# A two-branch linear-attention block: x's first 256 rows by transposing transfers, the first weights on one queue

## The chip, the cores and the metric

The kernel runs on one core of a Trainium2 chip. The metric is the device time of one execution in microseconds (us), lower is better. A profiled execution gives, beside its time, a span: from the first instruction that the profiler sees to the last.

## What is computed

The input x has 2048 rows of 640 numbers in bf16. Two linear-attention blocks A and B, each with its own weights, are applied to the same x, and a gate mixes their outputs row by row.

```python
def block(x, wqkv, wo):                       # 32 heads of 20
    q, k, v = split(x @ wqkv)                 # x: 2048x640, wqkv: 640x1920
    phi = lambda t: where(t > 0, t + 1, exp(t)) + 1e-6
    pq, pk = phi(q), phi(k)
    kv = einsum("bhsd,bhse->bhde", pk, v)     # per head 20x20
    z = einsum("bhsd->bhd", pk)
    o = einsum("bhqd,bhde->bhqe", pq, kv) / (einsum("bhqd,bhd->bhq", pq, z)[..., None] + 1e-6)
    return merge_heads(o) @ wo
g = sigmoid((x * gate_w).sum(-1, keepdims=True))
out = g * block(x, A_wqkv, A_wo) + (1 - g) * block(x, B_wqkv, B_wo)
```

## The kernel before

TensorE multiplies with the contracted dimension on the 128 partitions, so nearly everything needs x transposed: the tile `xT` holds it as 5 column groups (`c`) of 128 features by 2048 rows. The tile `xn` holds x as it is, 16 chunks of 128 rows, for later products with `pk`. Key weights of block A are in `wkA` (`wk[0]`, 5 groups by 640 columns, and two columns more, of which the first is filled with the gate weight), query weights in `wqA`, value weights in `wvA`.

The work starts with `k_first`: keys of block A for the first four row chunks. Each chunk takes 10 products on line 340 (5 groups `c` times two halves `hf` of the columns), added up in a bank pair `kA`. The second half is 321 columns wide: its last column is the gate. So the gate weights, loaded as 5 rows into the tile `g5` (`g` in the profile), are transposed by one small TensorE instruction (line 268, `gate_column`), and ScalarE copies them in three pieces into `wkA` (line 270) before any product with the second half can start.

Ahead of `k_first`, seven products of constants (`warm`, line 254) keep TensorE busy while the first transfers are on their way. Behind it come the first query products of block A (`qA`, lines 750 and 390) and from there an order written out by hand (the table `FIRST`), in which key chunks and query units follow each other to the end of the span's first third. Each engine works its list off in order.

How x's first rows come into `xT`: chunks 0 and 1 are loaded as they are into `xn` (line 200), one from SyncE's queue (SP) and one from ScalarE's (ACT); `x_transpose` lets TensorE transpose each by 5 products with the identity (line 295) into PSUM, and VectorE copies the result in two pieces to `xT` (line 298). Chunks 2 and 3 come by one transposing transfer of 256 whole rows (line 206, SP), rows 512 to 1023 by five transposing transfers of one column group each, the rest by two of 512 whole rows, all on SP. The key weights are loaded in pieces of 1, 1, 1 and 2 groups (line 203): the first, third and fourth from SP, the second from ACT. The gate weights come behind it on ACT. Chunks 2 and 3 are loaded into `xn` once more, untransposed, behind all of these (line 1313), then the other twelve (line 1315).

An instruction that starts a transfer occupies its queue for the time of the issue; the bytes land later. A queue's transfers wait in line for the 16 DMA engines, which both queues share.

Of the kernel before, what the change touches and what calls it, by code (L numbers as in the profile page):

```python
# [9 lines left out]
P = 128  # L10
# [5 lines left out]
S, D, H = 2048, 640, 32  # L16
Dh = D // H
DT = D // P
ST = S // P
NB = 4  # L20
CB = 4
HB = 512
# [56 lines left out]
def kernel(  # L79
# [11 lines left out]
    nc = tc.nc  # L91
    x2 = A_x.flatten_outer_dims()
# [28 lines left out]
    def ps_raw(name, slot=None):  # L121

        if slot is None:
            slot = turn[0]
            turn[0] = (slot + 1) % 4
        return pools.get(slot, pools["ps"]).tile([P, 4 * HB], BF16, tag=f"ps{slot}", name=name)

    def banks(raw):

        return raw.bitcast(FP32).rearrange("p (b n) -> p b n", b=2)  # L130

    def ps(name, slot=None):

        return banks(ps_raw(name, slot))

    xT = persist.tile([P, DT, S], BF16, name="xT")
    xn = persist.tile([P, ST, D], BF16, name="xn")
# [6 lines left out]
    ident = persist.tile([P, P], BF16, name="ident")  # L144
# [46 lines left out]
    nc.vector.memset(tiny[:], LOGS * EPS)  # L191
    nc.vector.memset(maskE[:], 1.0)
    nc.vector.memset(E4[0:2 * H, HF:D], 0.0)
    xb0 = x2[0:CB * P, :].rearrange("(q p) d -> p q d", p=P)
    wk = [None, None]
    wv = [None, None]
    wq = [None, None]
    wk[0] = wpool.tile([P, DT, D + 2], BF16, tag="wk", name="wkA")
    def load_x(eng, lo, hi):
        eng.dma_start(out=xn[:, lo:hi, :], in_=xb0[:, lo:hi, :])  # L200

    def load_wk(eng, lo, hi):
        eng.dma_start(out=wk[0][:, lo:hi, 0:D], in_=wq_dram[0][:, lo:hi, D:2 * D])

    def load_xT(lo, hi, c0=0, c1=DT):
        nc.sync.dma_start_transpose(out=xT[:, c0:c1, lo:hi], in_=x2[lo:hi, c0 * P:c1 * P])

    wq[0] = wpool.tile([P, DT, D], BF16, tag="wq", name="wqA")
    with tc.manual_schedule():
        load_x(nc.sync, 0, 1)  # L210
        load_x(nc.scalar, 1, 2)
        load_wk(nc.sync, 0, 1)
        load_wk(nc.scalar, 1, 2)
        nc.scalar.dma_start(out=g5[:], in_=gate_w.rearrange("(c p) -> c p", p=P))
        load_wk(nc.sync, 2, 3)
        load_wk(nc.sync, 3, DT)
        load_xT(HB // 2, HB)
        nc.scalar.preload_act_table_set("natural_log_exp_and_others")
        for lo, hi in ((0, 2), (2, 4), (4, DT)):
            nc.sync.dma_start(out=wq[0][:, lo:hi, :], in_=wq_dram[0][:, lo:hi, 0:D])  # L220
        for c in range(DT):
            load_xT(HB, 2 * HB, c, c + 1)
        for n in range(2, NB):
            load_xT(n * HB, (n + 1) * HB)
# [3 lines left out]
    for r in range(4):  # L228
# [3 lines left out]
        out=spread[:].rearrange("p (h t) -> p h t", t=TW), in_=I4[:, :, None].to_broadcast([P, H, TW])  # L232
    )
    for lo in range(0, HF, K6):
        part = maskE[:, lo:min(lo + K6, HF)]
        for sign, base in ((1, 0), (-1, Dh - 1)):
            nc.gpsimd.affine_select(
                out=part, in_=part, pattern=[[-sign * Dh, part.shape[1] // Dh], [0, Dh]],
# [3 lines left out]
    for rows, n in ((slice(0, 2 * H), H // 2), (slice(2 * H, P), H)):  # L242
        nc.gpsimd.tensor_copy(
            out=E4_rows[rows, 0:n], in_=I4[rows, 0:n, None].to_broadcast([rows.stop - rows.start, n, Dh])
# [20 lines left out]
    def gate_column(pt):  # L265

        at = slice(4 * HB - 2 * P, 4 * HB - 2 * P + DT)
        nc.tensor.transpose(out=pt[:, at], in_=g5[:], identity=ident[0:DT, 0:DT])
        for lo, hi in ((0, 1), (1, 2), (2, DT)):
            nc.scalar.copy(out=wk[0][:, lo:hi, D:D + 1], in_=pt[:, at, None][:, lo:hi])  # L270
# [18 lines left out]
                out=ge[32 * j:32 * j + 32], in_=by_rows[j][None].to_broadcast([H, 2, HB])  # L289
            )  # L290

    def x_transpose(i, slot):
        pt = ps_raw("xt", slot)
        for c in range(DT):
            nc.tensor.transpose(out=pt[:, c * P:(c + 1) * P], in_=xn[:, i, c * P:(c + 1) * P], identity=ident[:])
        src = pt[:, 0:D].rearrange("p (c n) -> p c n", c=DT)
        for lo, hi in ((0, 2), (2, DT)):
            nc.vector.tensor_copy(out=xT[:, lo:hi, i * P:(i + 1) * P], in_=src[:, lo:hi])

    class Phi:  # L300

        def __init__(self, dst, src, lifted=False):
# [35 lines left out]
    def k_mm(b, i, c, pt, hf):  # L338
        n = HF + (b == 0 and hf == 1)
        nc.tensor.matmul(  # L340
            pt[:, hf, 0:n], lhsT=xT[:, c, i * P:(i + 1) * P], rhs=wk[b][:, c, hf * HF:hf * HF + n],
            start=(c == 0), stop=(c == DT - 1),
        )
# [17 lines left out]
    def k_first():  # L361

        pts = []

        def part(i, cs, hfs=(0, 1)):
            for c in cs:
                for hf in hfs:
                    k_mm(0, i, c, pts[i], hf)

        x_transpose(0, 3)  # L370
        x_transpose(1, 2)
        gate_column(warm_raw)
        pts += [ps("kA", 1), ps("kA", 3)]
        for hf in range(2):
            for i in range(2):
                part(i, (0, 1), (hf,))
        for cs in ((2,), (3, 4)):
            for i in range(2):
                part(i, cs)
        pts += [ps("kA", 0), ps("kA", 2)]  # L380
        for i in range(2, CB):
            part(i, range(DT))
        return pts
# [148 lines left out]
    class PhiSteps:  # L532
# [9 lines left out]
        def part(self, t, k):  # L542
            return t if len(self.srcs) == 1 else t[:, k]
# [766 lines left out]

    with tc.manual_schedule():
        pts = k_first()
        nc.sync.dma_start(out=xn[:, 2:CB, :], in_=xb0[:, 2:CB, :])
        for n in range(1, NB):
            nc.sync.dma_start(
                out=xn[:, n * CB:(n + 1) * CB, :], in_=x2[n * HB:(n + 1) * HB, :].rearrange("(q p) d -> p q d", p=P)
            )
# [3 lines left out]
        lo, hi = GT  # L1321
# [197 lines left out]
        part = [slice(n * RB, (n + 1) * RB) for n in range(4)]  # L1519
# [70 lines left out]
        for i in range(1, half):  # L1590
            p, after = pairs[i], pairs[i + 1] if i + 1 < half else None
# [7 lines left out]
            q = after if i + 2 < half else p if after is None else None  # L1599
# [42 lines left out]
```

## Time and profile before

| | |
|---|---|
| time, median of 3 runs | 181.27 us (180.89, 181.27, 181.69) |
| profiled execution: its own time and its span | 180.88 us, 179.2 us |
| TensorE (PE) busy | 175.1 us, 98% of the span, 1266 products |
| VectorE (DVE) busy | 151.1 us, 84% |
| ScalarE (ACT) busy | 112.4 us, 63% |
| GpSimd (POOL) busy | 4.4 us, 2% |
| moved by DMA | 19.18 MB, mean 107 GB/s |

The profiled execution ran 0.39 us below the median, and 1.7 us of its time lie outside of its span. The busy time of TensorE counts overlapping products once; it says that TensorE is the engine that the others keep up with, not that it runs at its peak. PEld is the loading of the stationary operand, which runs beside the products.

### The profile page before, as it was taken

What the parts mean: (1) busy time and instruction counts of PE and PEld (TensorE: products, weight loads), DVE (VectorE), ACT (ScalarE), POOL (GpSimd) and SP (SyncE); (2) the same over time, 40 slices, a digit from 0 to 9 for tenths busy, and PEclk for the clock granted to TensorE, in tenths of its full rate; (3) what the DMA queues carried; (4) which work ended last, traced back from release to release, by engine and by line L of the source; (5) the groups of instructions that cost most, each with busy time, mean ns of one, the idle gap of its engine ahead of it and who ended that gap; (6) DMA issues with size and microseconds to landing.
All of it is one profiled execution on the core that took longest, in us unless ns stands there. A gap on an engine that the chain in (4) does not pass through costs nothing.

```text
span 179.2 us, 3362 instructions
## 1 busy us (share of the span) xinstructions
PE 175.1 (98%) x1266; PEld 116.2 (65%) x1266; DVE 151.1 (84%) x283; ACT 112.4 (63%) x235; POOL 4.4 (2%) x19
## 2 busy tenths in 40 slices
PE   7999999999999999999999999999999999999993
PEld 3666665665666577565656676766678777777772
DVE  2389999999999986898999997987988988686774
ACT  2388978999652453686869677674715756456410
POOL 7100000000000000000000000000000000000000
PEclk9999999999999999999999999999999999999999
DMA  5999999406045033000000033234802560233132
GB/s 174 293 188 178 214 366 316 108 4 183 3 125 180 0 116 121 0 0 0 2 4 2 0 72 114 57 103 157 233 3 70 145 154 0 74 113 113 73 134 90
DMA packets 22642, 19.18 MB, mean 107 GB/s; under 512 B 10338, under 2 KB 22114, under 8 KB 22626
## 3 DMA queue, kind: packets, MB, share of 16 engines
q1 hardware_dynamic: 22040, 18.47, 37.4%
q10 hardware_dynamic: 586, 0.49, 0.9%
q8 instruction: 10, 0.16, 0.4%
q14 instruction: 6, 0.05, 0.1%
HBM read 11.86 MB, written 4.80 MB: 93 GB/s over the span
## 4 chain that ended last, share of the span: by engine, by line
PE 95%; DMA 2%; DVE 1%; ACTq 0%; issue 0%
PE q L524 16%; PE kA L340 12%; PE kB L340 9%; PE gs L842 9%; PE gs L1331 9%; PE oy L1126 6%; PE oz L1126 5%; PE ox L1126 5%; PE ow L1126 4%; PE kB L524 3%; PE gB L812 2%; PE gA L812 2%; PE qA L390 2%; DMA g<-in_gate_w_dram 2%; PE q L390 1%; PE qA L750 1%
## 5 line engine op out<-in xcount | busy, mean ns | idle before, releaser
L340 PEld LDWEIGHTS <-xT 128*128 128x128 bf16 x280 | 27.1, 97 | 15.1 <-DMA xT<-in_A_x_dram 0.3
L340 PE MATMUL kA<-wkA,xT 128*128 128x320 bf16 (+1 forms) x160 | 24.0, 299 | 0.0
L554 DVE TENSOR_SCALAR e<-e 128x640 bf16<-128x640 bf16 (+2 forms) x59 | 19.2, 335 | 4.8 <-ACT e L548 4.5
L548 ACT ACTIVATE e<-q 128x512 bf16<-128x512 f32 x32 | 18.5, 599 | 5.7 <-PE q L524 5.2
L340 PE MATMUL kB<-wkB,xT 128*128 128x320 bf16 x120 | 19.2, 299 | 0.0
L548 ACT ACTIVATE e<-kB 128x640 bf16<-128x640 f32 (+1 forms) x18 | 11.4, 647 | 7.3 <-PE kB L524 3.2
L548 ACT ACTIVATE e<-kA 128x640 bf16<-128x640 f32 x16 | 11.3, 712 | 4.5 <-PE kA L340 3.8
L530 DVE TENSOR_TENSOR q<-q,p 128x512 f32<-128x512 f32 x16 | 11.1, 696 | 1.7 <-PE q L524 1.2
L561 DVE SCALAR_TENSOR_TENSOR pk<-kB,e 128x640 bf16<-128x640 f32 (+1 forms) x16 | 11.6, 736 | 0.5
L1126 PEld LDWEIGHTS <-xT 128*128 128x128 bf16 x85 | 8.1, 98 | 2.9
L1126 PEld LDWEIGHTS <-pqTA 128*128 128x128 bf16 x85 | 8.0, 98 | 2.8
L1126 PEld LDWEIGHTS <-pqTB 128*128 128x128 bf16 x80 | 7.8, 98 | 3.0
L524 PE MATMUL q<-xT,wqB 128*128 128x512 bf16 x32 | 9.7, 379 | 0.0
L1189 ACT COPY u<-ox 128x320 f32<-128x320 f32 x8 | 3.4, 425 | 9.7 <-PE ox L1126 9.7
L1131 DVE TENSOR_TENSOR osb<-oz,u 128x320 bf16<-128x320 f32 (+2 forms) x18 | 7.9, 451 | 1.9 <-PE oz L1126 1.6
L524 PE MATMUL q<-SQ,TM 128*128 128x512 bf16 x32 | 8.5, 379 | 0.0
L1331 PEld LDWEIGHTS <-xn 128*128 128x128 bf16 x64 | 6.1, 98 | 3.1 <-issue 0.7
L812 PEld LDWEIGHTS <-xn 128*128 128x128 bf16 x64 | 6.2, 98 | 2.8
L842 PEld LDWEIGHTS <-xn 128*128 128x128 bf16 x64 | 6.1, 98 | 2.9 <-issue 0.7
L561 DVE SCALAR_TENSOR_TENSOR pk<-kA,e 128x640 bf16<-128x640 f32 x8 | 6.6, 822 | 0.4
L561 DVE SCALAR_TENSOR_TENSOR pqTB<-q,e 128x512 bf16<-128x512 f32 x10 | 6.7, 683 | 0.0
L1126 PE MATMUL oz<-MB,xT 128*128 128x320 bf16 (+2 forms) x45 | 6.8, 284 | 0.0
(205 smaller groups left out, 372.6 us busy)
## 6 DMA issues: line engine op xcount, KB each, us to landing
out_dram<-osb SPq DMA_DIRECT2D x14, 160.0 KB, 1.8
xn<-in_A_x_dram SPq DMA_DIRECT2D x3, 640.0 KB, 7.8
wvA<-in_A_wqkv_dram SPq DMA_DIRECT2D x1, 800.0 KB, 10.4
wkB<-in_B_wqkv_dram SPq DMA_DIRECT2D x1, 800.0 KB, 4.6
wqB<-in_B_wqkv_dram SPq DMA_DIRECT2D x1, 800.0 KB, 5.8
wvB<-in_B_wqkv_dram SPq DMA_DIRECT2D x1, 800.0 KB
MA<-m_rows SPq DMA_DIRECT2D x1, 800.0 KB, 4.7
MB<-m_rows SPq DMA_DIRECT2D x2, 400.0 KB, 4.8
```

Of the source, the lines that this page charges most:

```text
L340: nc.tensor.matmul(pt[:, hf, 0:n], lhsT=xT[:, c, i * P:(i + 1) * P], rhs=wk[b][:, c, hf * HF:hf * HF + n], start=(c == 0), stop=(c == DT - 1),
L390: nc.tensor.matmul(dst, lhsT=mixed(wq[b][:, c, :], m), rhs=xT[:, c, n * HB:(n + 1) * HB], start=first, stop=last,)
L524: nc.tensor.matmul(dst, lhsT=left(c), rhs=right(c), start=first and k == 0, stop=last and k == len(cs) - 1, skip_group_check=not first,)
L530: nc.vector.tensor_tensor(out=dst, in0=acc, in1=sb, op=ALU.add)
L548: nc.scalar.activation(out=self.part(self.e, k), in_=self.srcs[k](), func=ACT.Exp)
L554: nc.vector.tensor_scalar(self.e, self.e, 1.0, EPS, op0=ALU.min, op1=ALU.add)
L561: nc.vector.scalar_tensor_tensor(out=self.part(self.dst, k), in0=src(), scalar=1.0 + EPS, in1=self.part(self.e, k), op0=ALU.add, op1=ALU.max,)
L812: nc.tensor.matmul(pt[:, hf, 0:HF], lhsT=xn[:, i, c * P:(c + 1) * P], rhs=pk[:, i, hf * HF:(hf + 1) * HF], start=(i == 0), stop=(i == ST - 1),
L842: nc.tensor.matmul(pt[:, n, 0:HF], lhsT=left[:, i, n * P:(n + 1) * P], rhs=right[:, i, :], start=(first and i == 0), stop=(i == hc - 1), s ...
L1126: nc.tensor.matmul(dst, lhsT=left[:, c, r0:r0 + P], rhs=right[:, c, :], start=(first and c == 0), stop=(c == DT - 1), skip_group_check=not ...
L1131: nc.vector.tensor_tensor(out=dst, in0=acc, in1=sb, op=ALU.add)
L1331: nc.tensor.matmul(dst[n], lhsT=left[:, i, n * P:(n + 1) * P], rhs=right[:, i, :], start=(first and i == 0), stop=(i == hc - 1), skip_grou ...
```

## The change

Three things are changed, all at the start of the program. The first 256 rows of x come into `xT` by two transposing transfers of 128 whole rows, at the head of SP's queue; `x_transpose`, its ten TensorE products and four VectorE copies are gone. All four pieces of the key weights and the gate weights are issued by ACT, in the order first and second piece, gate, third and fourth piece. And `k_first` has another order: two products of chunk 0's first half stand ahead of the gate's transposition, its second half and all of chunk 1 behind. The untransposed copy of chunks 0 and 1 in `xn` is loaded later, with chunks 2 and 3 in one transfer of 640 KB.

```diff
-    xb0 = x2[0:CB * P, :].rearrange("(q p) d -> p q d", p=P)
-    def load_x(eng, lo, hi):
-        eng.dma_start(out=xn[:, lo:hi, :], in_=xb0[:, lo:hi, :])
...
-        load_x(nc.sync, 0, 1)
-        load_x(nc.scalar, 1, 2)
-        load_wk(nc.sync, 0, 1)
+        load_xT(0, P)
+        load_wk(nc.scalar, 0, 1)
         load_wk(nc.scalar, 1, 2)
         nc.scalar.dma_start(out=g5[:], in_=gate_w.rearrange("(c p) -> c p", p=P))
-        load_wk(nc.sync, 2, 3)
-        load_wk(nc.sync, 3, DT)
-        load_xT(HB // 2, HB)
+        load_xT(P, 2 * P)
+        load_wk(nc.scalar, 2, 3)
+        load_wk(nc.scalar, 3, DT)
+        load_xT(2 * P, HB)
...
-    def x_transpose(i, slot):
-        pt = ps_raw("xt", slot)
-        for c in range(DT):
-            nc.tensor.transpose(out=pt[:, c * P:(c + 1) * P], in_=xn[:, i, c * P:(c + 1) * P], identity=ident[:])
-        src = pt[:, 0:D].rearrange("p (c n) -> p c n", c=DT)
-        for lo, hi in ((0, 2), (2, DT)):
-            nc.vector.tensor_copy(out=xT[:, lo:hi, i * P:(i + 1) * P], in_=src[:, lo:hi])
...
-        x_transpose(0, 3)
-        x_transpose(1, 2)
+        pts += [ps("kA", 1), ps("kA", 3)]
+        part(0, (0, 1), (0,))
         gate_column(warm_raw)
-        pts += [ps("kA", 1), ps("kA", 3)]
+        part(0, (0, 1), (1,))
         for hf in range(2):
-            for i in range(2):
-                part(i, (0, 1), (hf,))
+            part(1, (0, 1), (hf,))
...
-        nc.sync.dma_start(out=xn[:, 2:CB, :], in_=xb0[:, 2:CB, :])
-        for n in range(1, NB):
+        for n in range(NB):
```

On TensorE, right behind the `warm` products, this stood before (the end of the second chunk's transposition, the gate's transposition, the first key products; a DMAHW semaphore is the landing of one transfer, DVE, PE and Activation are work of these engines):

```order
L295 MATMUL xt<-ident,xn 128x128
L268 LDWEIGHTS g_89 [waits DMAHW4_49]
L268 MATMUL warm<-ident,g_89 128x5
L340 LDWEIGHTS xT [waits DVE_49]
L340 MATMUL kA<-wkA,xT 128x320 [waits DMAHW3_49]
L340 LDWEIGHTS xT
L340 MATMUL kA<-wkA,xT 128x320 [waits DMAHW2_49]
```

The gate's transposition came ahead of all key products, and four products of the first half stood between it and the first product that needs its column. At the same place, directly behind the last `warm` product, the changed program has (its line 328 is line 340 of before, 264 is 268):

```order
L328 LDWEIGHTS xT [waits DMAHW1_49]
L328 MATMUL kA<-wkA,xT 128x320 [waits DMAHW0_49]
L328 LDWEIGHTS xT
L328 MATMUL kA<-wkA,xT 128x320 [waits DMAHW2_49]
L264 LDWEIGHTS g_89 [waits DMAHW4_49]
L264 MATMUL warm<-ident,g_89 128x5 [waits Pool_49]
L328 LDWEIGHTS xT
L328 MATMUL kA<-wkA,xT 128x321 [waits Activation_49]
```

Two key products moved ahead of the gate, and the product right behind it now waits for ScalarE's copy.

SP's queue from its start, before:

```order
L200 DMA xn<-in_A_x_dram 128x640
L203 DMA wkA<-in_A_wqkv_dram 128x640 x2
L203 DMA wkA<-in_A_wqkv_dram 128x2x640
L206 DMA_TRANSPOSE xT<-in_A_x_dram 128x5x256
L220 DMA wqA<-in_A_wqkv_dram 128x2x640 [waits DMAHW0_49]
L220 DMA wqA<-in_A_wqkv_dram 128x2x640 [waits DMAHW1_49]
```

Four plain transfers stood ahead of the transposing one. The same queue in the changed program:

```order
L202 DMA_TRANSPOSE xT<-in_A_x_dram 128x5x128 x2
L202 DMA_TRANSPOSE xT<-in_A_x_dram 128x5x256
L216 DMA wqA<-in_A_wqkv_dram 128x2x640 [waits DMAHW0_49]
L216 DMA wqA<-in_A_wqkv_dram 128x2x640 [waits DMAHW1_49]
L216 DMA wqA<-in_A_wqkv_dram 128x640 [waits DMAHW2_49]
```

Only transposing transfers are left ahead of the query weights. ACT's queue in the changed program, from its start to the gate's copies:

```order
L199 DMA wkA<-in_A_wqkv_dram 128x640 x2
L209 DMA g_89<-in_gate_w_dram 5x128
L199 DMA wkA<-in_A_wqkv_dram 128x640
L199 DMA wkA<-in_A_wqkv_dram 128x2x640
L214 ACT_TABLE_LOAD
L266 COPY wkA<-warm 128x1 [waits PE_49]
```

Before, it held three transfers there: chunk 1 of x, the second piece of the key weights, and the gate; the table load followed at once.

## The prediction

> **What bounds the kernel now.** I read the page first: which engine is busy, and the chain of work that ended last.
>
> ```profile
> PE 175.1 (98%) x1266; PEld 116.2 (65%) x1266; DVE 151.1 (84%) x283; ACT 112.4 (63%) x235; POOL 4.4 (2%) x19
> PE 95%; DMA 2%; DVE 1%; ACTq 0%; issue 0%
> ```
>
> The chain is TensorE for 95% of the span. In order of time it shows where the rest lies (start, duration, what):
>
> ```profile
> 1.73 2.99 DMA g<-in_gate_w_dram
> ...
> 4.77 0.17 PE warm L268
> 4.94 5.75 PE kA L340 x40
> 10.70 0.86 PE qA L750 x4
> ...
> 14.48 0.82 PE kA L340 x6
> ```
>
> From 4.94 us on one product follows the other. So only the start counts: the change is worth what it moves the moment at which the 40 key products of `k_first` are done, now 10.70. The timeline shows what these wait for (start, duration, engine, idle time before):
>
> ```profile
> 0.84 2.87 PE L254 MATMUL warm<-const-bfloat16-1.0 128*128 128x512 bf16 x7 [0.84 <-PEq L1626]
> 3.65 0.73 PE L295 MATMUL xt<-ident,xn 128*128 128x128 bf16 x10
> 4.13 1.02 DVE L298 COPY xT<-xt 128x256 bf16<-128x256 bf16 x4 [2.62 <-PE xt L295]
> 4.77 0.17 PE L268 MATMUL warm<-ident,g 5*128 5x5 bf16 x1 [0.39 <-DMA g<-in_gate_w_dram]
> 7.76 2.60 PEld L340 LDWEIGHTS <-xT 128*128 128x128 bf16 x20 [0.29 <-DMA xT<-in_A_x_dram]
> 2.34 1.28 ACT L218 ACT_TABLE_LOAD   x1 [2.34 <-issue]
> 4.98 0.30 ACT L270 COPY wkA<-warm 128x1 bf16<-128x1 bf16 x3 [1.35 <-PE warm L268]
> ```
>
> The ten transpositions (3.65 to 4.38) and the first copies lie in the time until the gate weights land at 4.72: removing them frees no time on the chain by itself. Before chunks 2 and 3 TensorE waits 0.29 us for their transposing transfer. Without that wait 40 products take 5.75 - 0.29 = 5.46 us, 0.137 each.
>
> **What the transfers do.** Issues on SP, then on ACT, then time from issue to landing (last number):
>
> ```profile
> 1.26 1.37 SPq L203 DMA_DIRECT2D wkA<-in_A_wqkv_dram  x3
> 2.67 1.86 SPq L206 DMA_TRANSPOSE xT<-in_A_x_dram  x1
> 4.59 1.59 SPq L220 DMA_DIRECT2D wqA<-in_A_wqkv_dram  x3
> 0.81 0.41 ACTq L200 DMA_DIRECT2D xn<-in_A_x_dram  x1
> 1.25 0.46 ACTq L203 DMA_DIRECT2D wkA<-in_A_wqkv_dram  x1
> 1.73 0.58 ACTq L214 DMA_DIRECT2D g<-in_gate_w_dram  x1
> xn<-in_A_x_dram ACTq DMA_DIRECT2D x1, 160.0 KB, 3.0
> wkA<-in_A_wqkv_dram ACTq DMA_DIRECT2D x1, 160.0 KB, 3.7
> wkA<-in_A_wqkv_dram SPq DMA_DIRECT2D x1, 320.0 KB, 4.3
> xT<-in_A_x_dram SPq DMA_TRANSPOSE x1, 5.0
> wqA<-in_A_wqkv_dram SPq DMA_DIRECT2D x1, 320.0 KB, 5.1
> ```
>
> The 320 KB key piece, issued at about 2.2, lands at 6.5; the 256-row transposition, 2.67 + 5.0, at 7.7; the first query weights, 4.59 + 5.1, at 9.7. Every landing comes just ahead of its use: the start is a race of transfers, and the DMA engines are full (stretch, its length; the last two numbers are the engines' busy share and GB/s):
>
> ```profile
> 2.00:5.00 3.00, 2.61 (x17) 1.21 (x16) 0.86 (x4) 1.30 (x2) 2.74 (x12) 1.00 0.94 298
> 8.00:9.25 1.25, 1.25 (x11) 0.89 (x10) 1.06 (x2) 0.73 (x4) 0.00 (x0) 1.00 1.05 358
> 14.00:15.25 1.25, 1.25 (x10) 0.81 (x9) 1.25 (x3) 0.99 (x3) 0.00 (x0) 1.00 0.85 134
> 15.25:16.75 1.50, 1.50 (x10) 0.85 (x9) 1.50 (x5) 1.28 (x4) 0.00 (x0) 1.00 1.27 290
> ```
>
> Plain query weights move at 358 GB/s (second row), whole-row transpositions at 134 in their first stretch and 290 once they run (third and fourth).
>
> **The change part by part.**
>
> *Transpositions by TensorE and VectorE's copies go*: 0.73 and 1.02 us of busy time, off the chain as shown, 0 us. They also filled TensorE between `warm` and the first key product; what that may cost is a rival below.
>
> *SP's issues.* Longer transposing issues, and a short one's landing in a nearly empty queue:
>
> ```profile
> 11.34 1.26 SPq L206 DMA_TRANSPOSE xT<-in_A_x_dram  x1
> 12.64 2.99 SPq L206 DMA_TRANSPOSE xT<-in_A_x_dram  x1
> 15.67 3.58 SPq L206 DMA_TRANSPOSE xT<-in_A_x_dram  x1
> xT<-in_A_x_dram SPq DMA_TRANSPOSE x1, 2.8
> ```
>
> 256 whole rows take 1.86 us to issue, 512 take 2.99 to 3.58; a straight line through 1.86 and 3.58 gives 1.0 us for 128 rows (estimate; 1.3 by the line through 2.99). Two of them and the 256 rows occupy SP from 0.81 to 0.81 + 2.0 + 1.86 + gaps = 4.75, against 4.59: everything behind is issued 0.16 us later. Its cover: the first query weights land at 9.7 and are used at 10.70; the last column group (issue 11.34, landed 14.1) is used in the last two of the six products from 14.48, at 15.0. Both keep over 0.5 us, so 0 us.
>
> *Chunk 0's landing.* No 128-row transposition stands in the trace. Below: the 512x128 one above, 2.8 us from issue, four fifths of the bytes in a quiet queue: 3.6. Above: the 256 rows' 5.0, behind 800 KB on its queue: 5.8. The new one heads its queue but shares the engines with ACT's weights, so it is nearer to the first: 3.3 us, 4.1 (taken; 3.6 to 4.6 for the likely part).
>
> *The first key pieces and the gate on ACT.* The first key piece takes the place of x's chunk 1: 0.81 + 3.0 = 3.8. The second and the gate keep issue time and bytes ahead of them (320 KB before the gate): 4.95 and 4.72 by the rows, somewhat earlier if SP, which by 2.6 us had issued 800 KB and now has issued 160, leaves them more. I take 4.6 for both (4.2 to 4.95).
>
> *The new wait.* After two products and the gate's transposition (4.65 or so) TensorE stands until ScalarE has copied the column; all of chunks 0 to 3 is queued behind. From transposition to copy it was 4.98 - 4.77 = 0.21, the first of three copies takes somewhat over 0.1 of the 0.30, and the semaphores some: TensorE goes on at 5.1. Before, at 4.94, four products covered this wait. ScalarE itself is free by then: five issues (0.41, 0.46, 0.58, 0.46, 0.46 with gaps, the 320 KB one like the others) end at 3.3, the table load of 1.28 at 4.6. Remaining: 38 products, 5.19 us, so 10.3 if nothing else is late.
>
> *Third and fourth key piece.* They are issued at 2.34 and 2.84, the fourth 0.65 us later than before. It is needed after ten more products, at 5.1 + 1.37 = 6.5. By its old 4.3 it lands at 7.1; against a slower SP queue ACT may get more of the engines, then 6.0. I take 6.7: a wait of 0.2.
>
> *Chunks 2 and 3.* Issued at 2.87 with only 320 KB ahead on SP: 7.9 at most by the old 5.0; at least issue end 4.75 and the 1.5 us by which the quiet one landed after its issue, 6.3. Taken: 7.2, needed at 7.7, so the old 0.29 us of waiting goes.
>
> *Chunks 0 and 1 untransposed, later.* 320 KB more behind the transpositions, 0.9 us at 358 GB/s. The last of these loads is issued at 21.0, and the first reader is VectorE at 34.5:
>
> ```profile
> L1315 SPq DMA_DIRECT2D xn<-in_A_x_dram x3: 469/505/505, 19.9 to 21.0; - x3
> L1062 DVE TENSOR_TENSOR S<-xn x2: 681/683/685, 34.5 to 40.4; 128x1024 bf16<-128x1024 bf16 x2
> ```
>
> Sum: 5.1 + 5.19 + 0.2 = 10.5, against 10.70: 0.2 us gained. The profiled execution would come to 180.88 - 0.2 = 180.7, and, 0.39 above as before, the median to 181.1.
>
> **Two rules against the rows.** By rows, transposed bytes are dearer than plain ones: 134 to 290 against 358 GB/s. The Trainium skill, "Advanced Engine Details and Errata", section "X-Bar Transpose (TRN2)", says that on this chip transposing transfers are as fast as regular ones; by that, the 328 KB now transposed cost the engines no more than before, and the fourth key piece would land at the early end, 6.0, without its 0.2 us of waiting. The trace does not agree, so the sum keeps the wait. Of the queues, the DMA part of the answer for 2 to 5 us says (packets, MB, share of the engines; q1 is SP, q10 ACT):
>
> ```profile
> q1 hardware_dynamic: 488, 0.56, 60.8%
> q10 hardware_dynamic: 298, 0.33, 33.7%
> ```
>
> The two queues together fill the engines; whatever ACT gets is taken from SP, so the move of the weights makes no bytes faster in total.
>
> **The rivals.**
>
> *Slower: the race is lost (0.13).* If transpositions that share the engines with plain transfers get only 95 GB/s (an estimate: 70% of the 134 that they had alone), 656 KB take 6.9 us from the end of the first issue, 1.8, and with 0.5 to land chunks 2 and 3 are there at 9.2. 20 products of 0.137 follow: 11.95, 1.25 us late, 182.5. It decides from a landing after 8.9. For it: 134 GB/s is a stretch without any competition. Against: the 256 rows landed at 7.7 in spite of 800 KB ahead.
>
> *Slower: TensorE at the low clock (0.14).* The first products are slow:
>
> ```profile
> L254 PE MATMUL warm<-const-bfloat16-1.0 128*128 128x512 bf16 x6 | 2.7, 623 | 0.8 <-PEq L1626 0.8
> L750 PE MATMUL qA<-xT,wqA 128*128 128x512 bf16 x3 | 0.8, 379 | 0.0
> ```
>
> 623 ns against 379 for the same shape, and 2.87 us for six and a half of them, 0.44 apart, against 0.86 us for four later, 0.215 apart. The transpositions at 3.65 already run at 0.07 apart: the speed doubled at about 3.6, after 2.7 us of unbroken work. Now TensorE is mostly idle from 3.71 to 5.1. Where the speed has not risen by 3.71, another 2.7 us of work at half speed follow from 5.1: 1.35 us lost against the forecast, 182.4. It decides where the rise misses the end of `warm`. For it: the rise came only just ahead of that end. Against: in this execution it did come. The Trainium skill, "TensorE: Matmul & The Clock Gate", "Part 1: The HAM clock gate", says that the window which decides this runs freely, so that the rise falls differently from run to run; no row of one execution can show that.
>
> *Faster by more (0.11).* Everything at its early end or a little before: chunk 0 at 3.6, second piece and gate at 4.1, the fourth piece at 5.9, chunks 2 and 3 at 6.5. TensorE goes on at 4.55, and 38 products end at 9.75: 0.95 us gained, 180.3. It counts as faster from a gate at 4.15 on. Against: the gate's landing, 4.72, stood behind the same 320 KB of its own queue.
>
> *Nothing is moved at all:* that the removed work was off the chain is part of the forecast.
>
> **How the numbers follow.** Forecast, within 0.5% (0.9 us, about what a measurement of this kernel can tell from no change): 0.62. The two slower rivals together 0.27, the faster one 0.11. The range goes from just below the faster rival's price, 180.2, to 182.6, just beyond both slower rivals' prices; the rest of these, and what is faster still, is left out.
>
> **What would show it.** Right: first key product at 4.3 to 4.7, a gap of 0.3 to 0.5 us behind the gate's transposition that ScalarE's copy ends, the fourth key piece landing at 6.5 to 7.1 with a short wait in the middle of the key products, no wait for chunks 2 and 3, and `qA` at 10.3 to 10.9. Wrong: `qA` after 11.6 or before 9.8, key products 0.27 us apart, a wait of over 1 us for a transposing transfer, or a new wait further on, for column groups or query weights that I gave as covered.

## The result, and the profile after

| | before | after |
|---|---|---|
| time, median (lowest to highest) of 4 runs | 181.45 us (180.89 to 181.69) | 186.97 us (186.05 to 187.76) |
| ratio to before, 95% interval | | 1.0306 [1.0273, 1.0339] |
| profiled execution: its time and its span | 180.88 us, 179.2 us | 186.05 us, 184.3 us |
| start of the first query products (`qA`) | 10.70 us | 15.88 us |

The change made the kernel slower by 3.1%, outside the forecast's range. Of the kernel after, the page's shares of the chain by engine, then the chain's first pieces (start, duration, what):

```profile
PE 93%; DMA 4%; SPq 1%; DVE 1%; issue 0%
0.81 1.32 SPq L202
2.19 6.85 DMA xT<-in_A_x_dram
9.03 0.05 issue
9.08 6.80 PE kA L328 x36
15.88 0.22 PE qA L737
```

A DMA stands in the chain where TensorE's start was. It is the second transfer on SP, x's chunk 1: issued at 2.19, landed at 9.04. Behind it 36 key products still wait, of which the first starts at 9.08. From `qA` on nothing is lost: from its start to the end of the execution's time there are 186.05 - 15.88 = 170.17 us, and before there were 180.88 - 10.70 = 170.18.

The timeline of TensorE in the kernel after (start, duration, line, idle time before and what ended it):

```profile
0.84 2.93 PE L250 MATMUL warm<-const-bfloat16-1.0 128*128 128x512 bf16 x7 [0.84 <-PEq L1612]
4.96 0.71 PE L328 MATMUL kA<-wkA,xT 128*128 128x320 bf16 x2 [1.18 <-DMA xT<-in_A_x_dram]
5.60 0.18 PE L264 MATMUL warm<-ident,g 5*128 5x5 bf16 x1
6.04 0.69 PE L328 MATMUL kA<-wkA,xT 128*128 128x321 bf16 x2 [0.25 <-ACT wkA L266]
9.08 6.80 PE L328 MATMUL kA<-wkA,xT 128*128 128x320 bf16 x36 [2.35 <-DMA xT<-in_A_x_dram]
```

Three waits stand where the ten transpositions were: 1.18 us for chunk 0, 0.25 for ScalarE's copy of the gate, 2.35 for chunk 1. And the 36 products take 6.80 us, where 36 times the 0.137 of before is 4.93: in the trace they stand 0.267 us apart until about 12.5, twice the spacing of before, which is the low clock.

The transfers of the kernel after: three issues on SP (start, duration), then time from issue to landing of chunk 0, of chunks 2 and 3, and of the 320 KB key piece:

```profile
0.81 1.32 SPq L202 DMA_TRANSPOSE xT<-in_A_x_dram  x1
2.19 1.25 SPq L202 DMA_TRANSPOSE xT<-in_A_x_dram  x1
3.49 2.10 SPq L202 DMA_TRANSPOSE xT<-in_A_x_dram  x1
xT<-in_A_x_dram SPq DMA_TRANSPOSE x1, 4.1
xT<-in_A_x_dram SPq DMA_TRANSPOSE x1, 6.4
wkA<-in_A_wqkv_dram ACTq DMA_DIRECT2D x1, 320.0 KB, 6.1
```

Chunk 0 lands at 0.81 + 4.1 = 4.9, chunks 2 and 3 at 9.9, the key piece (issued at about 2.8) at 8.9. All are late. What moved meanwhile, per 2 us (stretch, length, five engines, granted clock, share of the DMA engines, GB/s); first before, then after:

```profile
5.00:7.00 2.00, 2.00 (x16) 1.38 (x15) 0.15 (x1) 0.28 (x3) 0.40 (x1) 1.00 1.20 282
7.00:9.00 2.00, 2.00 (x15) 1.25 (x14) 0.81 (x2) 1.43 (x4) 0.00 (x0) 1.00 1.07 315
```

```profile
5.00:7.00 2.00, 1.48 (x5) 0.39 (x5) 0.00 (x0) 0.30 (x3) 0.40 (x1) 1.00 1.11 205
7.00:9.00 2.00, 0.00 (x0) 0.00 (x0) 0.00 (x0) 0.00 (x0) 0.00 (x0) 1.00 1.28 157
```

The DMA engines are about as full as before (1.11 and 1.28 against 1.20 and 1.07), and they move a quarter to a half less. The DMA part of the answers for 3 to 5 us splits it by queue (packets, MB, share of the engines; q10 is ACT, q1 SP), before and then after:

```profile
q1 hardware_dynamic: 377, 0.43, 69.1%
q10 hardware_dynamic: 206, 0.21, 30.3%
```

```profile
q10 hardware_dynamic: 255, 0.29, 67.3%
q1 hardware_dynamic: 388, 0.09, 23.8%
```

ACT's plain bytes cost 0.303 x 2 us / 0.21 MB = 2.9 us of all engines per MB before, and 0.673 x 2 / 0.29 = 4.6 after, beside the transposing transfers, which in turn get only 45 GB/s (0.09 MB in 2 us).

### The profile page after: what moved, and what is told of

Same layout as the page of the kernel before. It is cut to its first block, busy times and chain, and to the rows that moved or that the text cites. A ratio compares the mean times of both kernels' runs of the same rounds, so it can differ in the third digit from the quotient of the medians.

```text
span 184.3 us, 3328 instructions
## 1 busy us (share of the span) xinstructions
PE 176.4 (96%) x1246; PEld 116.5 (63%) x1256; DVE 150.1 (81%) x279; ACT 112.3 (61%) x235; POOL 4.4 (2%) x19
## 4 chain that ended last, share of the span: by engine, by line
PE 93%; DMA 4%; SPq 1%; DVE 1%; issue 0%
PE q L511 15%; PE kA L328 13%; PE kB L328 9%; PE gs L829 8%; PE gs L1317 8%; PE oy L1113 6%; PE oz L1113 5%; PE ox L1113 4%; PE ow L1113 4%; DMA xT<-in_A_x_dram 4%; PE kB L511 3%; PE gB L799 2%; PE gA L799 2%; PE qA L377 2%; PE q L377 1%; PE qB L377 1%
## 5 line engine op out<-in xcount | busy, mean ns | idle before, releaser
L328 PEld LDWEIGHTS <-xT 128*128 128x128 bf16 x280 | 27.8, 100 | 20.7 <-DMA xT<-in_A_x_dram 4.8
L328 PE MATMUL kA<-wkA,xT 128*128 128x320 bf16 (+1 forms) x160 | 26.4, 317 | 3.8 <-DMA xT<-in_A_x_dram 3.5
L1113 PEld LDWEIGHTS <-xT 128*128 128x128 bf16 x85 | 8.1, 98 | 2.9
```

The lines of the kernel that those rows point to most:

```text
L328: nc.tensor.matmul(pt[:, hf, 0:n], lhsT=xT[:, c, i * P:(i + 1) * P], rhs=wk[b][:, c, hf * HF:hf * HF + n], start=(c == 0), stop=(c == DT - 1),
L1113: nc.tensor.matmul(dst, lhsT=left[:, c, r0:r0 + P], rhs=right[:, c, :], start=(first and c == 0), stop=(c == DT - 1), skip_group_check=not ...
```

## The experiments

Theory M: transposing transfers on one queue and plain ones on the other, in flight together, slow each other. Theory B: the transposing transfers hold each other up, standing back to back. Theory of the clock: TensorE's waits drop or delay the high clock, and this adds to the late data. A smaller rival was that transposed rows are dearer by themselves.

All runs, each against the kernel before on the same chip. The last columns are from the profiled execution; `qA` starts where the last key product of `k_first` ends (10.70 and 170.2 in the kernel before):

| run | median us | ratio [95%] | `qA` starts | own time less `qA` |
|---|---|---|---|---|
| the change | 186.97 | 1.0306 [1.0273, 1.0339] | 15.88 | 170.2 |
| e1 | 185.51 | 1.0244 [1.0196, 1.0292] | 15.59 | 170.2 |
| e2 | 184.24 | 1.0182 [1.0147, 1.0217] | 14.92 | 170.5 |
| e3 | 187.67 | single run | 17.50 | 170.2 |
| e4 | 186.94 | 1.0290 [1.0227, 1.0353] | 16.77 | 170.2 |
| e5 | 182.34 | 1.0036 [1.0002, 1.0071] | 11.25 | 170.9 |
| e6 | 182.37 | 1.0053 [1.0037, 1.0070] | 12.11 | 170.3 |
| e7 | 183.22 | 1.0097 [1.0071, 1.0123] | 13.67 | 170.3 |
| e8 | 184.52 | 1.0174 [1.0145, 1.0203] | 14.76 | 170.3 |
| e9 | 181.29 | 0.9994 [0.9977, 1.0012] | 11.47 | 170.3 |
| e10 | 183.81 | 1.0111 [1.0056, 1.0166] | 13.71 | 170.2 |
| e11 | 182.97 | 1.0096 [1.0074, 1.0117] | 11.98 | 170.2 |
| e12 | 185.66 | 1.0231 [1.0186, 1.0277] | 14.39 | 170.3 |

The last column is nearly constant. So these kernels are decided at their start, as the prediction read it, and can be judged by when `qA` starts. The one exception is e5, which loses another 0.7 us behind it, in waits for later column groups.

**e1: the kernel before, only with the queues' loads exchanged.** Its two chunks still come plain and are transposed by TensorE; SP carries x alone, ACT the weights.

```diff
         load_x(nc.sync, 0, 1)
-        load_x(nc.scalar, 1, 2)
-        load_wk(nc.sync, 0, 1)
+        load_wk(nc.scalar, 0, 1)
         load_wk(nc.scalar, 1, 2)
         nc.scalar.dma_start(out=g5[:], in_=gate_w.rearrange("(c p) -> c p", p=P))
-        load_wk(nc.sync, 2, 3)
-        load_wk(nc.sync, 3, DT)
+        load_x(nc.sync, 1, 2)
+        load_wk(nc.scalar, 2, 3)
+        load_wk(nc.scalar, 3, DT)
         load_xT(HB // 2, HB)
```

> Weights on ScalarE's queue as in the change, but x's chunks 0 and 1 plain (both from SyncE's queue) and transposed by TensorE as before; one transposing transfer of 256 rows. Theory M (a transposing transfer on one queue and plain transfers on the other, in flight together, slow each other): the 256-row transfer lands at 8.5 us or later, the fourth key piece later than 7.5, the first query products start at 11.5 to 13, time 182 to 184. Theory B (a transposing transfer directly behind another one is held up, whatever else runs): there is no such pair here, the 256 rows land at 6.5 to 7.5, query products at 10.5 to 11, time within 0.3% of before.

In e1, issue to landing of the 256-row transposition and of the last key piece, the stretches from 5 to 9 us, the queues from 5 to 7 us, and the last key products:

```profile
xT<-in_A_x_dram SPq DMA_TRANSPOSE x1, 8.9
wkA<-in_A_wqkv_dram ACTq DMA_DIRECT2D x1, 320.0 KB, 7.7
5.00:7.00 2.00, 1.68 (x10) 1.07 (x11) 0.62 (x3) 0.30 (x3) 0.40 (x1) 1.00 1.09 239
7.00:9.00 2.00, 1.52 (x7) 0.72 (x6) 0.00 (x0) 0.00 (x0) 0.00 (x0) 1.00 1.20 162
q10 hardware_dynamic: 299, 0.36, 68.9%
q1 hardware_dynamic: 444, 0.11, 39.7%
10.47 5.11 PE L340 MATMUL kA<-wkA,xT 128*128 128x320 bf16 x28 [0.35 <-DMA wkA<-in_A_wqkv_dram]
```

With no transposition behind another, and no byte more transposed than before, most of the loss is there: 8.9 us where the same transfer had 5.0, and 239 and 162 GB/s from full engines. B can't explain it, nor can dearer rows. The wait that ends last is the one for the fourth key piece, and plain bytes are dearer here too: ACT's 0.36 MB cost 0.689 x 2 / 0.36 = 3.8 us of all engines per MB, SP's transposed 0.11 MB cost 7.2. The time lies above the 182 to 184 that M gave. The clock, which M's sum had left out, is the rest as far as the key products show it: 28 of them take 5.11 us, where 28 times 0.137 is 3.84.

**e2: the change with all its transfers in one line.** The key weights go to SP, between the transposing transfers (T0, two pieces, T1, two pieces, T2); ACT has the gate alone.

```diff
-        load_wk(nc.scalar, 0, 1)
-        load_wk(nc.scalar, 1, 2)
+        load_wk(nc.sync, 0, 1)
+        load_wk(nc.sync, 1, 2)
...
-        load_wk(nc.scalar, 2, 3)
-        load_wk(nc.scalar, 3, DT)
+        load_wk(nc.sync, 2, 3)
+        load_wk(nc.sync, 3, DT)
```

> All of the change's transposing transfers stay, but the key weights stand between them on SyncE's queue; ScalarE's queue issues the gate weights alone. No two queues with data in flight, no two transposing transfers back to back. Theory M: chunk 1 lands at about 6.5, the last 256 rows at about 9 to 9.5 (their issue comes later), query products at 12 to 12.5, time 182.5 to 183.2. Theory B says the same of this order. If it is as slow as the change (over 185.5), both fall, and 128-row transposing transfers are dear by themselves.

In e2, landings of chunk 0, chunk 1, and chunks 2 and 3, then the key products:

```profile
xT<-in_A_x_dram SPq DMA_TRANSPOSE x1, 3.0
xT<-in_A_x_dram SPq DMA_TRANSPOSE x1, 3.4
xT<-in_A_x_dram SPq DMA_TRANSPOSE x1, 4.4
6.76 8.16 PE L328 MATMUL kA<-wkA,xT 128*128 128x321 bf16 x38 [0.25 <-ACT wkA L266]
```

In one line a 128-row transposition lands in 3.0 and 3.4 us, where the change took 4.1 and 6.85. This half went as M says. The time did not: 38 products take 8.16 us instead of 5.2, more than half of them at the low clock, which ends at 12.5 in the trace. And in e2 too a stretch with full engines moves little: 176 GB/s at a share of 0.98 from 5 to 7 us.

**e3: all three transposing transfers first, then the key weights, all on SP.**

```diff
+        nc.scalar.dma_start(out=g5[:], in_=gate_w.rearrange("(c p) -> c p", p=P))
         load_xT(0, P)
-        load_wk(nc.scalar, 0, 1)
-        load_wk(nc.scalar, 1, 2)
-        nc.scalar.dma_start(out=g5[:], in_=gate_w.rearrange("(c p) -> c p", p=P))
         load_xT(P, 2 * P)
-        load_wk(nc.scalar, 2, 3)
-        load_wk(nc.scalar, 3, DT)
         load_xT(2 * P, HB)
+        load_wk(nc.sync, 0, 1)
+        load_wk(nc.sync, 1, 2)
+        load_wk(nc.sync, 2, 3)
+        load_wk(nc.sync, 3, DT)
```

> The three transposing transfers of the change, then the key weights, all on SyncE's queue; ScalarE issues the gate weights alone. The weights come late, so the time says little (185 to 187 by both); the landings count. Theory M: with no plain transfer beside them chunk 0 lands by 4.2, chunk 1 by 5.5, the last 256 rows by 7.5. Theory B: chunk 0's landing comes over 1 us behind its data, chunk 1 lands after 6.5 and the last 256 rows after 8.5, as the second waits for the first's end.

In e3, issue to landing of chunk 0 and of chunk 1, and four stretches in which the number ahead of the last two is the granted clock; in the first of them the 256 rows move:

```profile
xT<-in_A_x_dram SPq DMA_TRANSPOSE x1, 2.9
xT<-in_A_x_dram SPq DMA_TRANSPOSE x1, 2.9
5.00:7.00 2.00, 0.00 (x0) 0.00 (x0) 0.00 (x0) 0.00 (x0) 0.40 (x1) 1.00 1.03 205
7.00:8.00 1.00, 0.00 (x0) 0.00 (x0) 0.00 (x0) 0.00 (x0) 0.00 (x0) 0.80 0.94 250
10.00:11.00 1.00, 1.00 (x5) 0.54 (x5) 0.00 (x0) 0.04 (x1) 0.00 (x0) 0.50 0.95 298
14.00:15.00 1.00, 1.00 (x8) 0.61 (x7) 0.33 (x1) 0.88 (x3) 0.00 (x0) 0.79 1.27 260
```

Without plain transfers beside them the 128 rows land in 2.9 us, and the second 128, right behind the first, in 2.9 as well: chunk 1 is there at 2.19 + 2.9 = 5.1, where the change had it at 9.04. The last packet of the 256 rows ends at 6.95 in the trace, and their semaphore is full at 7.5. M had given 5.5 and 7.5 as latest times for the two, B over 6.5 and over 8.5: B falls here. The transposed rows are not cheap for that: from 5 to 7 us, with 0.33 of 0.41 MB transposed, full engines move 205 GB/s, which is 1.03 x 2 / 0.41 = 5.0 us of all engines per MB against 2.9 for plain bytes. For the 0.33 MB that the change transposes in addition this makes 0.7 us of the engines (an estimate), so dearer rows are a part of the loss, and not the main one. In company the transposed bytes cost 7.2 (e1).

The clock of e3, by the trace's own records, is 1.00 from 4.2 to 7.6, 0.50 from there to 14.4, and 1.00 again (0.80 over a slice is 0.6 us at 1.00 and 0.4 at 0.50). The Trainium skill, "TensorE: Matmul & The Clock Gate", "Part 1: The HAM clock gate", says that the clock is decided anew at windows of about 3.4 us which run freely; the 3.4 us at 1.00 and the 6.8 us at 0.50 agree, as one and two of them. It also fits them that the clock stayed low for over four us after TensorE's unbroken work had begun at 9.95.

**e4 and e8: the change, with TensorE kept busy.** Products of constants that nothing reads are added: four more behind the first seven and 13 ahead of chunk 1's first product in e4, five more and seven in e8.

```diff
-    for n in [HB] * 6 + [RB]:
+    for n in [HB] * 6 + [RB] + [HB] * 4:
...
+        for _ in range(13):
+            nc.tensor.matmul(warm[:, 0, :], lhsT=one_l, rhs=one_r, start=True, stop=True)
```

> The change with more products of constants that nothing reads: four behind the first seven and thirteen ahead of chunk 1's first product. The transfers are the change's own. If 1.9 us of the loss are TensorE at its low clock (36 products in 6.80 us, where 36 took 4.92 before), the 36 products behind chunk 1's landing now take 4.9 to 5.2 us and the time falls by 1.5 to 2.0 us, to about 185.2. If the slow products have another cause (operands still landing, the weights' own arrival), they stay 0.19 apart and the time stays at 187.

> The change, with fewer unread products than before, so that they end ahead of chunk 1's landing: five behind the first seven, seven ahead of chunk 1's first product. The 36 products start at 9.0 to 9.9 and take 4.9 to 5.4 us, query products at 14.0 to 15.0, time 185.0 to 186.0: what is left above before is the transfers' part, the rest the clock's.

The added products and the 36 key products, e4 and then e8:

```profile
7.24 4.57 PE L363 MATMUL warm<-const-bfloat16-1.0 128*128 128x512 bf16 x13
11.66 5.11 PE L328 MATMUL kA<-wkA,xT 128*128 128x320 bf16 x36
```

```profile
6.69 1.69 PE L363 MATMUL warm<-const-bfloat16-1.0 128*128 128x512 bf16 x7
9.64 5.12 PE L328 MATMUL kA<-wkA,xT 128*128 128x320 bf16 x36 [1.26 <-DMA xT<-in_A_x_dram]
```

In both the 36 products take 5.1 us in place of 6.80. In e4 the gain was given back: the 13 unread products ran in part at the low clock themselves, and took until 11.66, 2.6 us past chunk 1's landing in the change. The trace of e4 has the clock at 0.50 from 7.05 to 10.46, in spite of the added work ahead; one of its four runs took 184.66 us, and whether the clock held there is not shown. That miss is why e8 has fewer. There the time falls from 1.0306 to 1.0174, 1.3% or 2.4 us: the clock's part, on medians. The profiled execution of the change, its lowest run, shows 1.87. e8's median lies below the 185.0 to 186.0 that were expected.

The transfers of the change, e4 and e8 are the same, and yet chunk 0 lands 4.1, 5.2 and 4.8 us behind its issue in the three profiles, and chunk 1 at 9.04 in the change and at 9.59 in e8. So about 1 us between two single landings means nothing here.

**e5 and e6: the kernel before, with 320 KB more.** The plain rows of chunks 2 and 3 are loaded early, on ACT in e5, on SP ahead of the transposing transfer in e6; the later load of the same rows goes.

```diff
+        load_x(nc.scalar, 2, CB)
...
-        nc.sync.dma_start(out=xn[:, 2:CB, :], in_=xb0[:, 2:CB, :])
```

> The kernel before, and the untransposed load of chunks 2 and 3 (320 KB, which it makes later anyway) is issued early from ScalarE's queue, at about 3.9 us, so that it is in flight with the transposing transfer of the same rows. Theory M: that transfer, which landed at 7.7, lands at 9 or later, by more than the 0.9 us that 320 KB take at 358 GB/s; query products start at 11.9 or later, time 182.4 to 183.5. If only the bytes count, it lands at 8.6 at most, query products at 11.5, time 182.0.

> The same 320 KB, but issued from SyncE's queue right ahead of the transposing transfer (whose issue then waits for a landing at 3.8 and starts 1.2 us later than before). Theory M: no mixing, only bytes: it lands at 8.4 to 8.8, query products at 11.4 to 11.7, time 181.8 to 182.3, faster than the run with the other queue by 0.5 us or more. If the bytes alone count, the two runs are equal.

In e5, DMA by queue from 5.5 to 7 us, and from 7.5 to 8.5:

```profile
q1 hardware_dynamic: 809, 0.30, 118.5%
```

```profile
q10 hardware_dynamic: 209, 0.26, 91.2%
q1 hardware_dynamic: 45, 0.02, 9.6%
```

Both cost about the same, 0.4% and 0.5%, so they do not tell M apart. The reason is in these rows: ACT's load, issued from 4.10 on, moved only when SP's transposing transfer was nearly done. The two were hardly in flight together, which was the point of e5. Inconclusive. (Of e5's loss, 0.7 us lie behind `qA`, so it isn't decided by its start alone.)

**e7: e2 with seven unread products** (four behind the first seven, two behind the first key product, one ahead of the gate's half).

```diff
-    for n in [HB] * 6 + [RB]:
+    for n in [HB] * 6 + [RB] + [HB] * 4:
...
-        part(0, (0, 1), (0,))
+        part(0, (0,), (0,))
+        fill(2)
+        part(0, (1,), (0,))
         gate_column(warm_raw)
+        fill(1)
```

> The one-line order (key weights between the transposing transfers on SyncE's queue), with seven more products of constants that nothing reads: four behind the first seven, two between the first two key products, one behind the gate's transposition. There, 38 key products took 8.16 us, about 2 us more than 5.2 and a wait for a transfer. If that is TensorE's low clock, the query products start at 12.6 to 13.0 (the last 256 rows land at 10.0, 20 products follow) and the time is 182.2 to 182.8. If not, 184.2 stays.

```profile
9.50 4.17 PE L328 MATMUL kA<-wkA,xT 128*128 128x320 bf16 x28 [0.95 <-DMA wkA<-in_A_wqkv_dram]
```

1.0 us is gained against e2, less than expected. The timeline of e7 gives the rest: at full speed TensorE now meets the fourth key piece 0.95 us early, a wait that the low clock had covered.

**e9: e1 with only the late key pieces back on SP**, ahead of the transposing transfer.

```diff
-        load_wk(nc.scalar, 2, 3)
-        load_wk(nc.scalar, 3, DT)
+        load_wk(nc.sync, 2, 3)
+        load_wk(nc.sync, 3, DT)
         load_xT(HB // 2, HB)
```

> The run with the queues changed alone, but the third and fourth key piece are issued by SyncE again, ahead of the transposing transfer; ScalarE keeps the first two pieces and the gate, all plain beside plain. In that run the 256 rows landed at 10.6 and the fourth key piece at 10.5. Theory M: with ScalarE's queue empty before the transposition's data move, these land at 7.3 to 8.2 and 6.3 to 7.0, the query products start at 10.5 to 11.2, time 181.0 to 182.0. If the loss of that run comes from something else in it (chunk 1 on SyncE's queue, the first piece on ScalarE's), it stays above 184.

```profile
xT<-in_A_x_dram SPq DMA_TRANSPOSE x1, 5.0
5.00:7.00 2.00, 2.00 (x12) 1.17 (x11) 0.63 (x3) 0.30 (x3) 0.42 (x1) 1.00 1.17 299
```

The transposing transfer of e9 lands in 5.0 us again, the engines move 299 GB/s, and the time is that of before (0.9994). 480 KB of key weights beside the transposing transfer, rather than ahead of it, are worth the whole 2.4% of e1. This is the case's strongest pair: same bytes, same kinds of transfers, and only two key pieces on one queue or the other. The exchange also moves the transposing transfer's issue, from 1.73 in e1 to 2.67; what it does away with is that both kinds are in flight together.

**e10: the same edit on the change.** The third and fourth key piece go to SP, between chunk 1 and chunks 2 and 3; the two 128-row transfers stay back to back.

```diff
         load_xT(P, 2 * P)
-        load_wk(nc.scalar, 2, 3)
-        load_wk(nc.scalar, 3, DT)
+        load_wk(nc.sync, 2, 3)
+        load_wk(nc.sync, 3, DT)
         load_xT(2 * P, HB)
```

> The change itself, but the third and fourth key piece are issued by SyncE, behind the two 128-row transposing transfers and ahead of the 256-row one. Theory M: only the first two pieces and the gate are in flight beside the first transposition, so chunk 1 lands at 5.5 to 7 instead of 9, the query products start at 12.0 to 13.5 (with up to 2 us of low clock), time 182.5 to 184.5. If transposing transfers back to back are the cause, chunk 1 still lands after 8.5 and the time stays over 186.

```profile
6.97 6.74 PE L328 MATMUL kA<-wkA,xT 128*128 128x321 bf16 x38 [0.25 <-ACT wkA L266]
xT<-in_A_x_dram SPq DMA_TRANSPOSE x1, 4.1
```

Chunk 1's wait is gone, with chunk 0 and 1 as close behind each other as in the change: B falls here as well. Chunks 2 and 3 land at 4.61 + 4.1 = 8.7, not 9.9. Of the loss of 3.1%, 1.1% is left; chunk 0, which still shares the engines with ACT's first pieces, lands at 5.85 here, and the 38 products take 1.5 us more than at full speed.

**e11: e10 with seven unread products** (five behind the first seven, two ahead of the gate's half).

```diff
-    for n in [HB] * 6 + [RB]:
+    for n in [HB] * 6 + [RB] + [HB] * 5:
...
+        for _ in range(2):
+            nc.tensor.matmul(warm[:, 0, :], lhsT=one_l, rhs=one_r, start=True, stop=True)
```

> The change with the third and fourth key piece back on SyncE's queue (183.8 us) and seven unread products that keep TensorE busy: five behind the first seven, two behind the gate's transposition. If low clock and transfers beside transpositions are the two parts of the loss, 38 key products take 5.2 to 5.6 us instead of 6.6, the query products start at 12.1 to 12.7 and the time is 182.3 to 183.0, 0.8 to 1.5 us above before: what is left is the late start behind chunk 0's landing and the longer issues. If it stays at 183.8, the clock was no part of what that run still lost.

```profile
6.60 5.38 PE L328 MATMUL kA<-wkA,xT 128*128 128x321 bf16 x38
```

As expected, 182.97. No wait and no low clock is left behind 6.60. What is left of the loss, 1.0% or 1.7 us, is ahead of it: the remaining 38 products start at 6.60, where in the same view of the kernel before they did at 4.87 + 2 x 0.137 = 5.14. Of this, two unread products are 0.4. The intervals of e10 and e11 overlap, so once the late transfers are cured the clock's part can't be told from none.

**e12: e1 with no transposing transfer at the start.** Chunks 2 and 3 come plain on SP and TensorE transposes them too; all the weights are on ACT.

```diff
-        load_xT(HB // 2, HB)
+        load_x(nc.sync, 2, CB)
...
+        x_transpose(2, 0)
+        x_transpose(3, 2)
```

> The run with the queues changed alone, but chunks 2 and 3 too are loaded plain by SyncE and transposed by TensorE, so that no transposing transfer is in flight while ScalarE's weights are; the fourth key piece's issue then waits for a landing at 3.9. Theory M: plain beside plain from two queues keeps its rate, over 300 GB/s in each stretch of 2 us from 3 to 9 us, where that run had 239 from 5 to 7 and 162 from 7 to 9. If two queues at once are the cause, whatever they carry, the rate falls below 250 here as well. The time, 181.5 to 183.5, has TensorE's and VectorE's added transpositions in it.

Stretch and queues from 5 to 7 us in e12, and ACT's last two key issues:

```profile
5.00:7.00 2.00, 1.50 (x9) 0.74 (x10) 0.56 (x2) 0.95 (x4) 0.42 (x1) 1.00 1.05 365
q1 hardware_dynamic: 464, 0.56, 80.6%
q10 hardware_dynamic: 152, 0.17, 24.9%
2.34 2.00 ACTq L203 DMA_DIRECT2D wkA<-in_A_wqkv_dram  x2
```

The rates are as M said: two queues, both plain, move 365 GB/s together where e1 moved 239 in this stretch, and ACT's bytes cost 0.249 x 2 / 0.17 = 2.9 us per MB again. The time missed, 185.66 against 181.5 to 183.5: here the two issues took 2.00 us rather than 0.85, the fourth piece got behind query weights and landed at about 9.2, and four chunks' products waited for it. So e12 shows the rate, and its time says nothing on M.

## Why the prediction was wrong, step by step

Two steps failed: chunk 1's transposing transfer had no term in the sum, though 36 products waited for it (2.35 us, to 9.04), and the landings were sized as if transposing transfers kept their speed beside the other queue's plain ones, which they did not. The late data then brought on the low clock, which the sum had at nothing and only a rival had priced.

**What bounds the kernel: right.** The start of `qA` decides, in all runs but e5.

**The term that was missing: chunk 1's landing.** The sum went from chunk 0 to the fourth key piece to chunks 2 and 3; the second transfer of SP's queue had no landing of its own. It landed at 9.04 and is the wait in the chain: with 36 products of 0.137 behind it, `qA` could not start before 14.0. This alone is 3.3 of the 5.2 us in the profiled execution.

**The landings that were mis-sized.** Chunk 0: 4.1 expected, 4.9 measured, outside the likely part, inside the bounds. Fourth key piece: 6.7, measured 8.9. Chunks 2 and 3: 7.2, "7.9 at most", measured 9.9. Their bounds came from transpositions that ran alone or behind plain transfers of their own queue. No row of before had one run beside the other queue's plain transfers for long, and the 5.0 us were held to be an upper end for a busy start. The sentence that failed here is that the move "makes no bytes faster in total": it looked at a gain only. The total itself fell, from 282 and 315 GB/s to 205 and 157.

**The rule on transposing transfers.** The prediction weighed the rule of the Trainium skill, "Advanced Engine Details and Errata", "X-Bar Transpose (TRN2)", that they are as fast as regular ones, and kept the rows. The runs agree with the rule in the time to land of one transfer by itself (2.9 us in e3, 3.0 for a plain 160 KB in the profile before). They do not agree in the rate (205 GB/s in e3's mostly transposed stretch, 358 for plain bytes in the profile before), nor in company: 8.9 us in e1 against 5.0 in e9. A second rule fits where both queues are plain: the Trainium skill, "DMA: Bandwidth & Descriptors", "Issuing engines are not separate DMA queues", says that transfers of all issuing engines interleave on the same 16 engines, and that a second one saves issue time only. e12's 365 GB/s agree; of a loss such as e1's 162 the rule says nothing.

**SP's issues.** 1.0 us for 128 rows was an estimate from one of two lines; 1.32 and 1.25 were measured, as the other line had it (1.3), and 2.10 for 256 rows. The query weights, issued from 5.63 on rather than 4.75, were no longer covered for a `qA` at 10.5; at 15.88 it did not matter.

**The gate.** Right in kind: ScalarE's copy ends a gap of 0.25 us behind the gate's transposition. It ended at 6.04 and not 5.1, since chunk 0 came late.

**The rivals.** Both slower ones named what happened. "The race is lost" put 95 GB/s and the decision on chunks 2 and 3 (9.2; measured 9.9) and again passed over chunk 1; the transposing queue had 45 GB/s from 3 to 5 us, 70 from 5 to 7 and 115 from 7 to 9. "The low clock" was priced at 1.35 us; measured are 1.87 in the profile and 2.4 on medians. They were given as alternatives with 182.5 and 182.4, though the first brings on the second: a TensorE that waits 2.35 us for data is a TensorE without work. Added, they would have reached about 183.8, still short by the missing term.

**The account on medians,** of 3.06%, from the ratios: clock 1.3 (the change less e8), late key pieces beside the transposing transfers 0.8 (e8 less e11), later first products 1.0 (e11), the last two with overlapping causes. That removing TensorE's transpositions frees nothing was not tested by itself.

**Open.** Why the engines lose so much when both kinds are in flight from two queues, why e2's single queue moved only 176 GB/s for a stretch, and what in e5 held ACT's load back. No version tried was faster than the kernel before.

## What to carry to other kernels

Where a start is bound by transfers, keep plain transfers off the other queue while transposing ones are in flight. Here, late key weights ahead of the transposing transfer in its own line cost nothing (e9), and beside it on the other queue 2.4% (e1). One line by itself is no cure: with the two kinds by turns it cost 1.8% (e2). Give each transfer that has a reader on the chain its own landing in the sum, not only the first and the last of a queue. And a new wait on TensorE's data near its first work is to be priced twice, as late data and as a later high clock; filling it with unread products helps only if they end before the data land (e8 against e4).

## What the runs showed of the hardware

Transposing transfers of one queue beside plain ones of the other cost total throughput, not only shares: with the DMA share at 1.2, 162 GB/s (e1) where plain transfers had 365 at 1.05 (e12). Part of this is the kind itself, with 205 GB/s at 1.03 where most bytes were transposed and one queue moved them all (e3); the rest is that both got dearer together, from 2.9 to 3.8 or 4.6 us of all engines per MB for the plain bytes and from 5.0 to 7.2 for the transposed. In one trace, a plain load of ACT hardly moved until a transposing transfer that had been issued ahead of it on SP was nearly done (e5); in e1 and the change, plain loads of ACT did move beside such transfers.

The granted-clock column can read 1.00 where products run at half speed. It does so ahead of the trace's first clock record: in e10 that stands at 9.79, and there the products' spacing falls from 0.27 to 0.14 us. The trace of the change has no clock record at all. In it, from 9 to 11 us:

```profile
9.00:11.00 2.00, 1.92 (x8) 1.11 (x9) 0.00 (x0) 0.00 (x0) 0.00 (x0) 1.00 1.11 354
```

Only 8 products of 320 columns lie in 1.92 us, 0.267 apart, where 40 of before took 0.137 each. Near the program's start the spacing of products tells the clock; the column does not.
